# State products of both heads in one 128-column product, behind the half's masked-score products

## The chip, the cores and the metric

The kernel runs on one core of one Trainium2 chip. The metric is the device time in microseconds of one execution. A core has TensorE (in the profile PE, its weight loads PEld), VectorE (DVE), ScalarE (ACT), GpSimd (POOL) and the DMA queues, of which SyncE (SP) issues most here. Each engine works through its own instructions in the order written; semaphores tie the engines together.

## The reference

Decay attention in blocks, then a mixer. The shapes are 4 batches, 8 heads, 768 positions and 64 dimensions per head; the mixer has 256 token features and 1536 channel features.

```python
for b in range(nb):                      # blocks of 64 positions
    intra = einsum('bhic,bhjc->bhij', qb, kb) * Dmask      # masked scores
    intra = einsum('bhij,bhjd->bhid', intra, vb)
    inter = einsum('bhid,bhde->bhie', qb * lam_pow, kv_state)
    out[:, :, sl] = intra + inter
    kv_state = lam_block * kv_state + einsum('bhsd,bhse->bhde', kb * rev_pow, vb)
...
u = x + (relu(x.T @ w_tok1) @ w_tok2).T
return u + relu(u @ w_ch1) @ w_ch2
```

## The kernel before

The attention works on 16 **pairs**: one batch and two neighbouring heads (h = 0, 1), whose 64 dimensions fill 128 partitions. Positions are cut into 6 chunks of 128. The six chunks are two **halves** of three, g = 0 and 1.

For pair i, `scores` makes the 128x128 scores of every chunk and VectorE multiplies them by the decay mask (tile `a`, L299). `state` makes the products of decayed k with v (`kv`, L257), VectorE scans them over the chunks (`sv`, L265), and GpSimd places them in `st` (program name `stb`, L278): for every chunk 128x128, head 0's state in rows and columns 0 to 63, head 1's in 64 to 127, zeros elsewhere. GpSimd also scales q (`qs`, L244). `outputs(i, g)` then adds up in one PSUM bank `xT`, which has 3x128 columns, head h in partitions 64h to 64h+63: for every chunk and head the masked-score product (L314: v as weights, 64 columns, `a` streamed) and, but for chunk 0, the state product (L324: the head's 64 columns of `st` as weights, all 128 rows, `qs` streamed). ScalarE copies the bank to `uT` (L331). There is one `xT` bank, so the other half's first product waits for that copy.

The order is the one in which the code is written, for all engines. A pass of the loop over i issues: scores of pair i+1, `outputs(i, 0)`, the `kv` products of pair i+1, `outputs(i, 1)`, then transposes of k and q of pair i+2 (L208, L228; from pair 5 and 8 on VectorE and DMAs do these: L218, L221), then from pass 4 on pieces of the token mixer (`token_hidden` L449, `token_out` L469), with the transposes of the finished half (`turn_back`, L346) between them. In pass 15 there is no `kv`; a `token_hidden` stands between the two halves. Loads of later pairs and of the mixer's weights go through SP. The channel mixer (L640, L661) follows from about 179 us to the end.

Of the kernel before, what the change touches and what calls it, by code (L numbers as in the profile page):

```python
# [21 lines left out]
def kernel(  # L22
# [23 lines left out]
    nc = tc.nc  # L46
    B, H, S, D = q.shape
# [3 lines left out]
    P = 128  # L51
# [27 lines left out]
    def bank(tag, nm, n):  # L79
        return ps.tile([P, n], F32, tag=tag, bufs={"sc": 4, "xT": 1, "sh": 3}[tag], name=nm)  # L80
# [99 lines left out]
    for i in range(2):  # L180
        st = ap.tile([P, NC - 1, 2, D], F32, name=f"stb{i}")
# [7 lines left out]
    while n < P:  # L189
        nc.vector.tensor_mul(  # L190
            out=lamp[:, :, n : 2 * n], in0=lamp[:, :, 0:n], in1=lamp[:, :, n - 1 : n].broadcast_to([P, NP, n])
        )
        n *= 2
    for p in range(NP):
        nc.gpsimd.tensor_copy(
            out=keep[:, p, :, 1:], in_=lamp[:, p, P - 1 : P, None].broadcast_to([P, D, NC - 2])
# [3 lines left out]
    kTs, qTs, qss, kds, weights_of = {}, {}, {}, {}, {}  # L200
# [105 lines left out]
    def outputs(i, g):  # L306
        b, p = pairs[i]
        st = stb[i % 2]
        xT = bank("xT", f"xT{i}{g}", 3 * P)
        for cg in range(3):  # L310
            c = 3 * g + cg
            cs = slice(cg * P, (cg + 1) * P)
            for h in range(2):
                nc.tensor.matmul(  # L314
                    out=xT[h * D : (h + 1) * D, cs],
                    lhsT=vns[i][:, h, c, :],
                    rhs=weights_of[i, g, h][:, cg, :],
                    start=(cg == 0),
                    stop=False,
                )  # L320
            if c == 0:
                continue
            for h in range(2):
                nc.tensor.matmul(  # L324
                    out=xT[h * D : (h + 1) * D, cs],
                    lhsT=st[:, c - 1, h, :],
                    rhs=qss[i][:, c - 1, :],
                    start=False,
                    stop=(cg == 2),
                )  # L330
        nc.scalar.copy(out=uT[b][:, p, 3 * g * P : (3 * g + 3) * P], in_=xT)  # L331

    x_of = {}
# [221 lines left out]
    for i in range(-2, NI):  # L555
# [3 lines left out]
        if i >= 0:  # L559
            outputs(i, 0)  # L560
# [4 lines left out]
        if i >= 0:  # L565
            outputs(i, 1)
# [201 lines left out]
```

## Time and profile before

| | us |
|---|---|
| three runs | 600.35, 600.77, 603.7 |
| their median | 600.77 |
| the profiled execution | 602.27 |
| its span, first to last instruction | 600.5 |
| VectorE, ScalarE, GpSimd busy in the span | 349.3, 155.4, 139.0 |

In the profile a group of instructions is named by its line, engine and operation, then out<-in with the program's names, the part of the TensorE array that it uses (128\*64 is all 128 rows and 64 columns), the shape and the count. An fp32 matmul is recorded as two instructions (two passes), so that the 160 state products are x320. "Mean ns of one" is from start to modelled end; matmuls overlap, so their rate is read from starts.

### The profile page before, as it was taken

To read this page: it belongs to the slowest core of one execution; us is meant where nothing else is said; L and a number is where in the kernel's file an instruction comes from. 1 tells how busy PE (TensorE), PEld (TensorE's weight loads), DVE (VectorE), ACT (ScalarE), POOL (GpSimd) and SP (SyncE) were. 2 spreads that over 40 slices of the span, in tenths; PEclk is the share of its full clock that TensorE was granted. 3 is DMA by queue.
4 is the path that set the end of the run, shared out by engine and by line. 5 is a ranking of instruction groups with operands and counts; after the bars stand their busy time and mean duration, and the time that the engine had idled before them with its cause. 6 is when DMAs were issued, how large, how long until landed. Compare 5 with 4: busy or idle time off the path is not lost.

```text
span 600.5 us, 10671 instructions
## 1 busy us (share of the span) xinstructions
PE 581.5 (97%) x4378; PEld 566.3 (94%) x4378; DVE 349.3 (58%) x663; ACT 155.4 (26%) x322; POOL 139.0 (23%) x131
## 2 busy tenths in 40 slices
PE   5979899999999999999999999999999999999997
PEld 5868799889999999999999999999999999999996
DVE  4588777886733667446534664446534664356654
ACT  3454423444223243212201221012211221011011
POOL 5646533364215358201100010001100010000000
PEclk9989899999999999999999999999999999999999
DMA  9999899999100112011200111011200200016667
GB/s 186 240 229 172 140 175 164 191 175 161 37 11 27 37 36 70 1 33 38 71 1 0 61 47 35 1 36 41 66 1 0 71 1 1 0 21 90 89 90 134
DMA packets 169648, 44.73 MB, mean 74 GB/s; under 512 B 162816, under 2 KB 163968, under 8 KB 169600
## 3 DMA queue, kind: packets, MB, share of 16 engines
q1 hardware_dynamic: 165456, 42.88, 37.6%
q10 hardware_dynamic: 4144, 1.18, 0.9%
q8 instruction: 34, 0.56, 0.4%
q14 instruction: 14, 0.11, 0.1%
HBM read 37.75 MB, written 6.29 MB: 73 GB/s over the span
## 4 chain that ended last, share of the span: by engine, by line
PE 87%; DVE 6%; DMA 4%; ACT 2%; issue 1%; SPq 0%; ACTq 0%; DVEq 0%
PE ph L640 34%; PE po L661 33%; PE ph L449 6%; PE pu L469 4%; PE xT L314 3%; PE sc L290 3%; PE xT L324 2%; DMA kn<-in_k_dram 2%; DMA uT<-in_moe_w_tok_dram 2%; PE xp L346 1%; DVE xlo L355 1%; PE kv L257 1%; DVE uT L383 1%; DVE a L299 1%; DVE uT L389 1%
## 5 line engine op out<-in xcount | busy, mean ns | idle before, releaser
L645 DVE SCALAR_TENSOR_TENSOR hl<-ph,hh 128x384 fp32r<-128x384 f32 x96 | 53.5, 558 | 164.9 <-ACT hh L644 164.9
L661 PE MATMUL po<-hh,c2h 128*128 128x384 f32 x384 | 129.4, 337 | 0.0
L640 PE MATMUL ph<-uh,c1h 128*128 128x384 f32 x384 | 129.2, 337 | 0.0
L640 PE MATMUL ph<-ul,c1h 128*128 128x384 f32 x384 | 129.2, 336 | 0.0
L640 PE MATMUL ph<-uh,c1l 128*128 128x384 f32 x384 | 129.1, 336 | 0.0
L661 PE MATMUL po<-hh,c2l 128*128 128x384 f32 x384 | 128.8, 335 | 0.0
L661 PE MATMUL po<-hl,c2h 128*128 128x384 f32 x384 | 128.6, 335 | 0.0
L644 ACT ACTIVATE hh<-ph 128x384 fp32r<-128x384 f32 x96 | 47.3, 492 | 299.5 <-PE ph L640 297.8
L666 DVE TENSOR_TENSOR uT<-po,uT 128x384 f32<-128x384 f32 x192 | 104.7, 552 | 23.5 <-PE po L661 23.4
L661 PEld LDWEIGHTS po<-hh,c2l 128*128 128x128 f32 x384 | 72.1, 188 | 0.0
L640 PEld LDWEIGHTS ph<-ul,c1h 128*128 128x128 f32 x384 | 72.1, 188 | 0.0
L661 PEld LDWEIGHTS po<-hl,c2h 128*128 128x128 f32 x384 | 72.1, 188 | 0.0
L640 PEld LDWEIGHTS ph<-uh,c1h 128*128 128x128 f32 x384 | 72.1, 188 | 0.0
L661 PEld LDWEIGHTS po<-hh,c2h 128*128 128x128 f32 x384 | 72.0, 188 | 0.0
L640 PEld LDWEIGHTS ph<-uh,c1l 128*128 128x128 f32 x384 | 72.0, 188 | 0.0
L375 POOL TENSOR_TENSOR c1l<-wa,c1h 128x512 fp32r<-128x512 f32 x10 | 12.9, 1292 | 179.9 <-ACT c1h L374 179.9
L534 POOL TENSOR_TENSOR ul<-uT,uh 128x384 fp32r<-128x384 f32 x32 | 36.0, 1157 | 37.4 <-ACT uh L533 37.4
L314 PE MATMUL xT<-a,vn 128*64 128x128 f32 x384 | 37.1, 285 | 4.3 <-ACT uT L331 4.3
L278 POOL COPY stb<-sv 64x320 f32<-64x320 f32 x32 | 26.7, 834 | 43.6 <-DVE sv L265 42.7
L299 DVE TENSOR_TENSOR a<-sc,mask 128x384 f32<-128x384 f32 x64 | 31.2, 549 | 5.8 <-PE sc L290 5.7
L324 PE MATMUL xT<-qs,stb 128*64 128x128 f32 x320 | 32.0, 278 | 0.0
L314 PEld LDWEIGHTS xT<-a,vn 128*64 128x64 f32 x384 | 22.8, 139 | 8.3 <-ACT uT L331 4.7
(80 smaller groups left out, 756.9 us busy)
## 6 DMA issues: line engine op xcount, KB each, us to landing
raw<-in_moe_w_ch_dram SPq DMA_DIRECT2D x20, 512.0 KB, 3.6
vn<-in_v_dram SPq DMA_DIRECT2D x16, 384.0 KB, 5.4
kn<-in_k_dram SPq DMA_DIRECT2D x30, 192.0 KB, 5.3
out_dram<-y SPq DMA_DIRECT2D x108, 48.0 KB, 1.9
qn<-in_q_dram SPq DMA_DIRECT2D x44, 96.0 KB, 4.1
uT<-in_moe_w_tok_dram SPq DMA_DIRECT2D x2, 1536.0 KB, 8.5
kr<-in_k_dram SPq DMA_DIRECT2D x32, 96.0 KB, 4.1
uT<-in_moe_w_ch_dram SPq DMA_DIRECT2D x4, 512.0 KB, 5.3
```

The costliest lines, as they stand in the source:

```text
L278: nc.gpsimd.tensor_copy(out=st[r, :, h, :], in_=sv[r].rearrange("p (e c) -> p c e", c=NC - 1))
L299: nc.vector.tensor_mul(out=a, in0=sc[h].rearrange("p (c i) -> p c i", i=P), in1=mask[:, 2 * p + h, None, :].broadcast_to([P, 3, P]),)
L314: nc.tensor.matmul(out=xT[h * D : (h + 1) * D, cs], lhsT=vns[i][:, h, c, :], rhs=weights_of[i, g, h][:, cg, :], start=(cg == 0), stop=False,)
L324: nc.tensor.matmul(out=xT[h * D : (h + 1) * D, cs], lhsT=st[:, c - 1, h, :], rhs=qss[i][:, c - 1, :], start=False, stop=(cg == 2),)
L449: nc.tensor.matmul(out=ph, lhsT=w[:, c, fs], rhs=x[:, c], start=(i == 0), stop=(i == 3 * NC - 1))
L469: nc.tensor.matmul(out=pu, lhsT=h[:, kk, cs], rhs=w[:, kk, ss], start=(i == 0), stop=(i == 3 * NK - 1))
L534: nc.gpsimd.tensor_sub(out=ul[:, t], in0=ub[:, t], in1=uh[:, t].bitcast(F32))
L640: nc.tensor.matmul(out=ph, lhsT=w[:, ct, js], rhs=x[:, ct], start=(i == 0), stop=(i == 11))
L644: nc.scalar.activation(hh, ph, AF.Relu)
L645: nc.vector.scalar_tensor_tensor(out=hl, in0=ph, scalar=0.0, in1=hh.bitcast(F32), op0=ALU.max, op1=ALU.subtract)
L661: nc.tensor.matmul(out=po, lhsT=w[:, jj, cs], rhs=h, start=(i == 0), stop=(i == 3 * JG - 1))
L666: nc.vector.tensor_add(out=ub, in0=po, in1=ub)
```

## The change

In a half, the state products no longer stand between the chunks' masked-score products, one for each head. A loop of its own behind the three chunks makes them with one product per chunk for both heads: all 128 columns of `st` are the weights, and the result goes to all 128 partitions of `xT`. What is computed is the same, since the parts of `st` off the two blocks are zeros.

```diff
-            if c == 0:
-                continue
-            for h in range(2):
-                nc.tensor.matmul(
-                    out=xT[h * D : (h + 1) * D, cs],
-                    lhsT=st[:, c - 1, h, :],
-                    rhs=qss[i][:, c - 1, :],
-                    start=False,
-                    stop=(cg == 2),
-                )
+        for c in range(max(3 * g, 1), 3 * g + 3):
+            cs = slice((c - 3 * g) * P, (c - 3 * g + 1) * P)
+            nc.tensor.matmul(
+                out=xT[:, cs],
+                lhsT=st[:, c - 1].rearrange("p h d -> p (h d)"),
+                rhs=qss[i][:, c - 1, :],
+                start=False,
+                stop=(c == 3 * g + 2),
+            )
         nc.scalar.copy(out=uT[b][:, p, 3 * g * P : (3 * g + 3) * P], in_=xT)
```

The state product is L324 before and L323 in the changed kernel, whose lines behind it are one lower (L449 becomes L448). Only TensorE's order changes; the other engines and queues have the same instructions in the same order.

TensorE in pair 8, the end of half 0 and the step to half 1. `xT80` and `xT81` are the banks of the two halves, `a800` and `a801` the masked scores of the two heads; before:

```order
L314 MATMUL xT80_1383<-a801_1210,vn8_1036 64x128
L314 MATMUL xT80_1383<-a800_1208,vn8_1036 64x128
L314 MATMUL xT80_1383<-a801_1210,vn8_1036 64x128
L324 MATMUL xT80_1383<-qs8_1224,stb0_111 64x128 x2
L314 MATMUL xT80_1383<-a800_1208,vn8_1036 64x128
L314 MATMUL xT80_1383<-a801_1210,vn8_1036 64x128
L324 MATMUL xT80_1383<-qs8_1224,stb0_111 64x128 x2
L257 MATMUL kv9_1395<-vn9_1184,kd9_1290 64x64 x10
L314 MATMUL xT81_1408<-a810_1220,vn8_1036 64x128
```

and the same place in the changed kernel:

```order
L314 MATMUL xT80_1343<-a800_1173,vn8_1006 64x128
L314 MATMUL xT80_1343<-a801_1175,vn8_1006 64x128
L314 MATMUL xT80_1343<-a800_1173,vn8_1006 64x128
L314 MATMUL xT80_1343<-a801_1175,vn8_1006 64x128
L323 MATMUL xT80_1343<-qs8_1189,stb0_111 128x128 x2
L257 MATMUL kv9_1353<-vn9_1149,kd9_1250 64x64 x10
L314 MATMUL xT81_1366<-a810_1185,vn8_1006 64x128
```

Two products of 128 columns stand directly ahead of `kv` in the place of four of 64 columns; before them all products of the half have 64 columns, and `kv` behind them has 64 again.

TensorE in pair 8, the end of half 1 and the token mixer's first products behind it (`ph101`); before:

```order
L314 MATMUL xT81_1408<-a810_1220,vn8_1036 64x128
L314 MATMUL xT81_1408<-a811_1222,vn8_1036 64x128
L324 MATMUL xT81_1408<-qs8_1224,stb0_111 64x128 x2
L449 MATMUL ph101_1430<-xhi10_853,w1h_129 128x256
L449 MATMUL ph101_1430<-xhi10_853,w1l_130 128x256
```

and changed:

```order
L314 MATMUL xT81_1366<-a810_1185,vn8_1006 64x128
L314 MATMUL xT81_1366<-a811_1187,vn8_1006 64x128
L323 MATMUL xT81_1366<-qs8_1189,stb0_111 128x128 x3
L448 MATMUL ph101_1385<-xhi10_828,w1h_129 128x256
L448 MATMUL ph101_1385<-xhi10_828,w1l_130 128x256
```

The step from 64-column to 128-column products stood ahead of the mixer's products; it now stands three state products earlier.

## The prediction

> **What bounds the kernel now.** First the page: busy shares, then the chain that ended last.
>
> ```profile
> PE 581.5 (97%) x4378; PEld 566.3 (94%) x4378; DVE 349.3 (58%) x663; ACT 155.4 (26%) x322; POOL 139.0 (23%) x131
> PE 87%; DVE 6%; DMA 4%; ACT 2%; issue 1%; SPq 0%; ACTq 0%; DVEq 0%
> ```
>
> TensorE is 87% of the chain, so a change of its work counts, unless TensorE then waits less. The state products all lie before 179 us. The view by stretches shows how tight TensorE is there (columns: length, busy us and instructions by engine, granted clock, DMA).
>
> ```profile
> 20.60:54.00 33.40, 28.46 (x408) 24.84 (x408) 26.09 (x47) 16.79 (x38) 19.29 (x17) 0.95 1.02 228
> 76.00:182.00 106.00, 104.94 (x1224) 97.03 (x1221) 74.49 (x136) 37.13 (x81) 38.17 (x36) 1.00 0.81 131
> ```
>
> From 76 us on TensorE is busy 104.94 of 106 us: pairs 6 to 15 are bound by it. In 20.6 to 54 us it is free for some 5 us: pairs 1 to 4 run under another bound.
>
> Next the timeline of TensorE over pair 8 (start, length, line, part of the array, count).
>
> ```profile
> 98.83 0.66 PE L314 MATMUL xT<-a,vn 128*64 128x128 f32 x8
> 99.31 0.39 PE L324 MATMUL xT<-qs,stb 128*64 128x128 f32 x4
> 99.53 0.39 PE L314 MATMUL xT<-a,vn 128*64 128x128 f32 x4
> 99.75 0.39 PE L324 MATMUL xT<-qs,stb 128*64 128x128 f32 x4
> 99.97 0.75 PE L257 MATMUL kv<-vn,kd 128*64 128x64 f32 x20
> 100.72 0.44 PE L314 MATMUL xT<-a,vn 128*64 128x128 f32 x4
> ...
> 101.86 0.39 PE L324 MATMUL xT<-qs,stb 128*64 128x128 f32 x4
> 102.18 0.39 PE L449 MATMUL ph<-xhi,w1h 128*128 128x256 f32 x1
> 102.40 0.28 PE L449 MATMUL ph<-xhi,w1l 128*128 128x256 f32 x1
> 102.52 0.28 PE L449 MATMUL ph<-xlo,w1h 128*128 128x256 f32 x1
> ```
>
> Groups of four (two heads, two passes) start 0.22 us apart. The same timeline, cut to a narrow window, shows two of them, and the costliest groups have the length of one (count, busy us, mean ns):
>
> ```profile
> 99.42 0.28 PE L324 MATMUL xT<-qs,stb 128*64 128x128 f32 x2
> ...
> L324 PE MATMUL xT<-qs,stb 128*64 128x128 f32 x320 | 32.0, 278 | 0.0
> L257 PE MATMUL kv<-vn,kd 128*64 128x64 f32 x320 | 12.6, 223 | 1.1 <-ACT kd L237 0.6 <-POOL kd L239 0.5
> ```
>
> Two instructions together take 0.28 us, and one alone 278 ns, so **both heads' passes start together**, each on its half of the columns. A chunk's state product costs two passes of 0.11 us, not four.
>
> **What the change does to the passes.** The 128-column product has two passes as well, and each streams the same 128 columns of `qs`. The trace has no fp32 product of this form. Bounds: the weights of 128 columns and 128 streamed columns of the scores, twelve steps of two heads in 1.54 us, 0.13 each with the start-up in them and 0.12 with the 0.2 for it taken off (the entry price worked out below); on the other side half of 0.11, if four passes' work really went away. I take 0.11 per pass, the pace of L314 and L324, since the streamed side is the same and the scores' weights, as wide, hold their pace near it.
>
> ```profile
> 97.36 1.54 PE sc L290 x24
> ```
>
> **Gain in the passes: 0.** 160 instructions go, but their time lay beside the other head's.
>
> **What it adds: changes of the array's form.** The last L324 pass starts at 101.97 (0.11 after 101.86), the first L449 at 102.18: 0.21 where a pass takes 0.11. The second L449 follows after 0.22, where 0.12 is its pace (102.40 to 102.52): its weights are not loaded ahead. So entering the 128-column form costs 0.10 + 0.10 = 0.20 us. The Trainium skill, "TensorEngine Tiling (Array Packing)", Key Properties, says that a change of mode, as against a change of tile, drains the engine; the 0.21 here agrees, and it speaks against this change; it names no price. With transposes behind, entry is cheaper:
>
> ```profile
> 45.74 0.39 PE L324 MATMUL xT<-qs,stb 128*64 128x128 f32 x4
> 46.06 0.44 PE L208 MATMUL kt<-ident,kn 128*128 128x128 f32 x2
> ```
>
> 45.85 to 46.06 is again 0.21, but the second follows after 0.44 - 0.28 = 0.16, against 0.11 in steady state: 0.10 + 0.05, about 0.16 with rounding. For L323, a full product like L449 and not a transpose, I take 0.20; 0.16 is the lower end, and would take 0.4 off the sum below.
>
> Leaving the 128-column form is seen at pair 15:
>
> ```profile
> 172.91 0.28 PE L449 MATMUL ph<-xlo,w1h 128*128 128x256 f32 x1
> 173.12 0.66 PE L314 MATMUL xT<-a,vn 128*64 128x128 f32 x8
> ```
>
> 0.21 instead of 0.12, and eight instructions in 0.66 where four steps would give 3 x 0.11 + 0.28 = 0.61: 0.09 + 0.05 = 0.14 us.
>
> **Half 0, pairs 0 to 14**: one entry (0.20) before the state products and one exit (0.14) into `kv`, both new. The exit has cover. `kv`'s last pass starts at 100.50 (99.97 + 0.75, less 0.22 for the last one), and its steps are 0.06, so half 1 could start at 100.56; it starts at 100.72, behind ScalarE's copy of the one `xT` bank:
>
> ```profile
> 100.19 0.48 ACT L331 COPY uT<-xT 128x384 f32<-128x384 f32 x1 [2.41 <-PE xT L324]
> ```
>
> The copy ends at 100.67. It hangs on the last state product, not on `kv`, so 0.14 of exit goes into 0.16 of wait. Without that cover it would cost its 0.14. The scan behind `kv` comes 0.34 later, with the next pair's half 0 to use it several us on.
>
> **Half 1**: the entry that stood ahead of the next work moves three products up. Before L208 or L346 (pairs 0 to 5, 11, 12, 15) 0.20 replaces 0.16: +0.04. Before L449 or L469 (6 to 10, 13, 14) +0. **Pair 15**: no `kv`; in half 0 the entry moves only, 0. In half 1 the copy is awaited by a transpose, and the copy comes the whole 0.20 later:
>
> ```profile
> 178.81 0.31 PEld L346 LDWEIGHTS xp<-ident,uT 128*128 128x128 f32 x3 [0.34 <-ACT uT L331]
> ```
>
> **What waits swallow.** From the chain in order of time, the timeline of TensorE, and that of its weight loads:
>
> ```profile
> 20.59 9.87 DMA uT<-in_moe_w_tok_dram
> 35.08 0.69 PE L314 MATMUL xT<-a,vn 128*64 128x128 f32 x4 [2.22 <-ACT uT L331]
> 44.60 0.44 PE L314 MATMUL xT<-a,vn 128*64 128x128 f32 x4 [0.88 <-ACT uT L331]
> 52.48 0.44 PE L314 MATMUL xT<-a,vn 128*64 128x128 f32 x4 [1.23 <-ACT uT L331]
> 63.14 0.74 PE L257 MATMUL kv<-vn,kd 128*64 128x64 f32 x17 [0.48 <-POOL kd L239]
> 68.25 0.55 PE L346 MATMUL xp<-ident,uT 128*128 128x128 f32 x3 [2.20 <-DVE sv L265]
> 86.41 3.70 DMA qn<-in_q_dram
> 94.94 0.19 PEld L449 LDWEIGHTS ph<-xhi,w1h 128*128 128x128 f32 x1 [0.40 <-DVE uT L474]
> 117.29 6.57 DMA kn<-in_k_dram
> 129.49 0.31 PEld L346 LDWEIGHTS xp<-ident,uT 128*128 128x128 f32 x3 [0.56 <-issue]
> ```
>
> Pair 1 and half 0 of pair 2 lie beside the load of 20.59 and the conversion behind it, which end in the wait of 2.22; half 0 of pair 3 in 0.88; its half 1 and half 0 of pair 4 in 1.23; pair 5 in 0.48 and 2.20. Pairs 7 (about 88 us) and 10 (about 122) lie beside the loads of 86.41 and 117.29, with TensorE waiting 0.40 and 0.56 at their ends. Pair 0 stands before the load of 20.59 on the chain, and 6, 8, 9, 11 to 14 on TensorE's own stretch of it.
>
> **Sum.** Eight pairs at 0.20 = 1.6; five half 1s before transposes on the chain (0, 2, 4, 11, 12) at 0.04 = 0.2; pair 15 0.2: **+2.0 us**. On the profiled execution 602.27 + 2.0 = 604.3; it is 1.5 over the median of 600.77, so on the median **602.8**. Its own uncertainty: in two stretches the clock was granted at half,
>
> ```profile
> 34.66:38.07 3.41, 2.99 (x25) 2.66 (x26) 3.38 (x6) 0.48 (x2) 3.34 (x3) 0.50 0.93 182
> 68.80:72.20 3.40, 3.40 (x18) 3.40 (x18) 1.16 (x3) 1.51 (x3) 3.26 (x4) 0.50 1.19 150
> ```
>
> in the second with TensorE fully busy: 18 instructions in 3.40 us, at 0.12 each 2.2. One such stretch more or less is some 1.3 us, with the pass price of 0.12 for 0.11 (about 0.6 over the paying pairs) 1.5: 601.3 to 604.3.
>
> **Rivals.** *Fewer instructions are worth their time*: a pass costs an issue price, so a chunk falls from 0.22 to 0.11. Eight full pairs then give 8 x (0.55 - 0.20) = 2.8, the half 1s of 2 and 4 2 x 0.29, pair 15 0.35: -3.6 after the small terms, 597.2. The Trainium skill's same page, Instruction Overhead, has some 60 cycles for each matmul on TRN2, which points this way. Against: the two heads in 0.28 us, above. 6%.
>
> *Everything follows TensorE* (the slower side): the waits above are released by work that TensorE fed a few us before, so they move along instead of swallowing, and `kv`, late by 0.34, becomes what half 1 waits for. It decides where an exit costs over 0.16 or the delay between two waits exceeds the second (0.40 is the smallest). Then all 15 pairs pay 0.34, nine half 1s 0.04, pair 15 0.2: +5.6, 606.4. For it: 0.14 is close to 0.16. Against: the two loads and conversions of 2 to 10 us have their own length. 16%.
>
> *No weights ahead*: a full fp32 pass can't have the next weights loaded beside it, 0.22 instead of 0.11 for each pass after the first; about eight per pair and eight pairs +7, with half 1 of 2, 4 and 15 +8.4, so 611. Against: the scores at 0.12 with weights as wide. 4%.
>
> *No drain*: widening from 64 to 128 columns with the same rows costs nothing: 600.8. Against: 102.18. 4%.
>
> **Chances.** The forecast has 70%. A measurement tells 0.5% from no change, that is 3.0 us: 597.8 and 603.8. Of the forecast's range a sixth, 0.12, lies over 603.8. Slower: 0.12 + 0.16 + 0.04 = 0.32; same: 0.58 + 0.04 = 0.62; faster 0.06. The range reaches over the second rival and stops short of the first and third: 600.6 to 606.4.
>
> **What would show it.** L323 x160, starts 0.11 apart, 0.21 after the last L314 and 0.21 again to its second pass; `kv` 0.21 after the last L323; half 1's first L314 still 0.05 behind the copy's end; no change after 180 us. Wrong if L323 runs at 0.06 or 0.22 a pass, if half 1 starts behind `kv` alone, or if the waits at 35, 52, 68, 95 and 129 us keep their lengths while their ends move later.

## The result, and the profile after

| | us |
|---|---|
| changed kernel, 7 runs | 602.77 to 606.82, median 604.48 |
| kernel before, the 7 runs beside it | 599.93 to 603.7, median 600.77 |
| ratio | 1.0071, 95% interval 1.0046 to 1.0096 |
| the same comparison again (7 runs; 18 of before) | 1.0054, 1.0035 to 1.0073 |

The change makes the kernel slower by 4.3 us (2.8 to 5.8), or 3.2 (2.1 to 4.4) in the second comparison, each ratio taken on 600.77. The direction was forecast and the size was too small: +2.0. The median lies 0.7 us over 603.8, where the prediction had set the bound between no change (chance 0.62) and slower (0.32).

The profiled execution of the changed kernel took 604.34 us, its span is 602.6. The page's busy line and the chain:

```profile
PE 584.3 (97%) x4218; PEld 566.1 (94%) x4218; DVE 349.4 (58%) x663; ACT 154.7 (26%) x322; POOL 138.9 (23%) x131
PE 87%; DVE 5%; DMA 4%; ACT 1%; SPq 1%; POOL 0%; issue 0%; POOLq 0%
```

160 instructions are gone and TensorE is busy 2.8 us longer. The timeline of TensorE over pair 8, to be laid beside the one of before:

```profile
98.37 0.88 PE L314 MATMUL xT<-a,vn 128*64 128x128 f32 x12
99.18 0.71 PE L323 MATMUL xT<-qs,stb 128*128 128x128 f32 x4
99.82 0.80 PE L257 MATMUL kv<-vn,kd 128*64 128x64 f32 x20
100.46 0.88 PE L314 MATMUL xT<-a,vn 128*64 128x128 f32 x12
101.27 0.94 PE L323 MATMUL xT<-qs,stb 128*128 128x128 f32 x6
101.96 0.36 PE L448 MATMUL ph<-xhi,w1h 128*128 128x256 f32 x1
102.16 0.28 PE L448 MATMUL ph<-xhi,w1l 128*128 128x256 f32 x1
```

Half 0 takes 100.46 - 98.37 = 2.09 us, before 100.72 - 98.83 = 1.89: +0.20, as predicted. Half 1 to the mixer's second product takes 102.16 - 100.46 = 1.70, before 102.40 - 100.72 = 1.68. ScalarE's copy between the halves:

```profile
99.93 0.48 ACT L330 COPY uT<-xT 128x384 f32<-128x384 f32 x1 [2.60 <-PE xT L323]
```

It ends at 100.41 and half 1 starts at 100.46, 0.05 behind it as before. But `kv`'s last pass now starts at 100.40 (99.82 + 0.80 - 0.22), and with its step of 0.06 half 1 could start at 100.46 behind `kv` alone, too: both are ready together, the exit has filled the wait.

The clock differs between the two profiles, and any comparison of spans has to know it (stretches, columns as before):

```profile
34.30:37.70 3.40, 2.65 (x27) 2.31 (x27) 3.40 (x6) 1.57 (x5) 3.00 (x3) 1.00 1.29 220
68.41:71.82 3.41, 3.41 (x19) 3.41 (x18) 1.21 (x4) 1.47 (x4) 2.88 (x3) 0.50 1.32 163
```

The stretch at 34.66 that had half the clock before has all of it here. So the spans differ by 2.1 us only, while the timed runs differ by 3 to 4.

To see where TensorE loses time, take the start of each pair's first masked-score product (the first L314 behind its scores), in a kernel less in the kernel before, and from that the step from one pair to the next. This is what each pair costs (us):

```
pair                 6    7    8    9   10   11   12   13  14+15   sum
predicted          .20    0  .20  .20    0  .24  .24  .20    .40   1.68
changed            .25  .37  .21  .21  .38  .28  .26  .22    .43   2.61
changed, again     .25  .36  .21  .20  .35  .28  .26  .22    .43   2.56
half 1 alone       .01  .00  .01  .01  .02  .07  .08  .03    .21    .44
half 0 alone       .19  .36  .19  .19  .38  .20  .19  .21    .21   2.12
order alone        .03 -.01 -.01 -.01  .00  .00  .00  .03    .01    .04
```

The column 14+15 is the step from pair 14 to the channel mixer's first L661. Pairs 7 and 10 stand out. Pairs 0 and 1, which the table leaves out, cost 0.31 us each in both profiles of the changed kernel, where the prediction had 0.24 and 0.

The prediction also named waits (at 35, 52, 68, 95 and 129 us) that would show it wrong if they kept their lengths. These are they, with two more of its list, at the times of before and in us; those at 95 and 129 are waits of TensorE's weight loads:

```
wait at             35    44    52    63    68    95   129
before            2.22   .88  1.23   .48  2.20   .40   .56
changed           2.14   .64   .97  none  2.14   .49   .59
changed, again    2.22   .53   .96  none  2.14   .49   .58
```

Those at 44, 52 and 63 us gave up 0.24 to 0.48 us. Those at 35 and 68 kept their lengths to 0.08 us, and those at 95 and 129, the ends of pairs 7 and 10, got no shorter at all.

### The profile page after: what moved, and what is told of

It is laid out like the page before. It is cut to its first block, busy times and chain, and to the rows that moved or that the text cites. A ratio compares the mean times of both kernels' runs of the same rounds, so it can differ in the third digit from the quotient of the medians.

```text
span 602.6 us, 10351 instructions
## 1 busy us (share of the span) xinstructions
PE 584.3 (97%) x4218; PEld 566.1 (94%) x4218; DVE 349.4 (58%) x663; ACT 154.7 (26%) x322; POOL 138.9 (23%) x131
## 4 chain that ended last, share of the span: by engine, by line
PE 87%; DVE 5%; DMA 4%; ACT 1%; SPq 1%; POOL 0%; issue 0%; POOLq 0%
PE ph L639 33%; PE po L660 33%; PE ph L448 6%; PE pu L468 4%; PE xT L314 3%; PE xT L323 3%; PE sc L290 2%; DMA uT<-in_moe_w_tok_dram 2%; DMA qn<-in_q_dram 1%; PE kv L257 1%; PE xp L345 1%; DMA kn<-in_k_dram 1%; DVE a L299 1%; DVE xlo L354 1%; DVE uT L391 1%; DMA kr<-in_k_dram 1%
## 5 line engine op out<-in xcount | busy, mean ns | idle before, releaser
L314 PE MATMUL xT<-a,vn 128*64 128x128 f32 x384 | 28.1, 281 | 3.8 <-ACT uT L330 3.8
L330 ACT COPY uT<-xT 128x384 f32<-128x384 f32 x32 | 15.3, 479 | 60.4 <-PE xT L323 60.4
L448 PE MATMUL ph<-xhi,w1h 128*128 128x256 f32 x96 | 28.8, 300 | 0.5 <-DVE hl L453 0.3
```

The costliest lines, as they stand in the source:

```text
L314: nc.tensor.matmul(out=xT[h * D : (h + 1) * D, cs], lhsT=vns[i][:, h, c, :], rhs=weights_of[i, g, h][:, cg, :], start=(cg == 0), stop=False,)
L448: nc.tensor.matmul(out=ph, lhsT=w[:, c, fs], rhs=x[:, c], start=(i == 0), stop=(i == 3 * NC - 1))
```

## The experiments

All experiments but the repetition put the state products of one chunk into a function `states(cg)` and choose with two flags: `wide` takes one 128-column product in the place of two of 64 columns, `behind` calls it behind the half's masked-score products and not behind each chunk's. The kernel before is `False, False`, the change `True, True`. The cuts below are of this code (`...` marks what is left out).

**Order alone.** The state products behind the masked-score products, but still one per head:

```diff
+        wide, behind = False, True
...
+            if not behind:
+                states(cg)
+        if behind:
+            for cg in range(3):
+                states(cg)
```

> State products moved behind the half's masked-score products, but still two of 64 columns per chunk. Theory A (the price is changing the array's form, 128*64 to 128*128 and back): no form is changed more often than before, so +0 us, within 1 us of the kernel before; in the trace the half is 0.22 us per chunk and product as before. Rival B (the new order itself costs, since the bank's last products now hang on the states): +2 to +4 us, like the whole change.

602.51 us against 601.78, ratio 1.0011 (0.9989 to 1.0033). In the trace no late pair moves by over 0.04 us (last row of the table of pairs). A holds: the new order is free, so the cost is in the widening.

**Wide, in place.** One 128-column product behind each chunk's masked-score products:

```diff
+        wide, behind = True, False
```

> One 128-column state product per chunk, left in its old place behind that chunk's masked-score products, so that the form changes at every chunk. Theory A, with 0.20 us to enter and 0.14 us to leave: half 0 pays 0.34 + 0.20 (its last exit lies in the wait for the copy), half 1 0.34 + 0.34 + 0.04, some 1.24 us per pair; the ten to eleven pairs on TensorE's path give +13 to +14 us, all sixteen +19.5. Theory C (the 128-column pass itself is dearer, by 0.01 to 0.02 us, and the form is free): as the whole change, +2 to +4 us.

615.46 against 601.78, ratio 1.024 (1.0211 to 1.0269): +14.4 us, where A gave 13 to 14 and C 2 to 4. As many 128-column passes as in the change cost over three times as much, so the price is on the change of form. TensorE in half 0 of pair 8 and the step to half 1 (in the experiments' kernels the masked-score products are L339, the 128-column state products L318, the 64-column ones L327):

```profile
100.98 0.66 PE L339 MATMUL xT<-a,vn 128*64 128x128 f32 x8
101.57 0.49 PE L318 MATMUL xT<-qs,stb 128*128 128x128 f32 x2
101.99 0.44 PE L339 MATMUL xT<-a,vn 128*64 128x128 f32 x4
102.36 0.49 PE L318 MATMUL xT<-qs,stb 128*128 128x128 f32 x2
102.78 0.80 PE L257 MATMUL kv<-vn,kd 128*64 128x64 f32 x20
103.42 0.44 PE L339 MATMUL xT<-a,vn 128*64 128x128 f32 x4
```

103.42 - 100.98 = 2.44, 0.55 over the 1.89 of before; worked out had been 0.34 + 0.20.

**Half 1 alone, half 0 alone.** The change in one half, the old code in the other (one line for each kernel):

```diff
+        wide, behind = g == 1, g == 1
...
+        wide, behind = g == 0, g == 0
```

> Half 1 as in the change, half 0 as before. Half 1 ends in 128-column work anyway, so the form changes as often as before. Theory A: +0.04 us before transposes, 0 before the token mixer, 0.2 in pair 15: +0.4 us in all. Theory C (each 128-column pass dearer): three fifths of the change's cost, +1.2 to +2.6 us.

> Half 0 as in the change, half 1 as before. Theory A: 0.20 us in each pair that TensorE bounds and nothing for the exit, which lies in the wait for the copy: +1.6 us if waits swallow what the prediction says, +3 us if all 15 pairs pay; nearly the whole cost of the change either way. Theory C: two fifths of the change's cost, +0.8 to +1.7 us.

Half 1: 603.08 against 601.78, 1.0019 (0.9995 to 1.0042). Half 0: 605.86, 1.0069 (1.0048 to 1.0089), all of the change's cost, +4.1 us (2.9 to 5.3). In the table the two rows add up to the changed kernel's sum: 0.44 + 2.12 = 2.56. Theory C, with three and two fifths, falls by half 0, whose interval begins over C's 1.7; half 1's, -0.3 to 2.5, would allow it. A's +3 for half 0, "if all 15 pairs pay", lies in the interval, but the pairs do not pay alike: pairs 7 and 10 cost 0.36 and 0.38, from half 0.

**Why pairs 7 and 10.** VectorE around pair 10, and the wait of TensorE at the pair's end, before and in the changed kernel:

```profile
123.12 0.82 DVE L265 TENSOR_TENSOR_SCAN sv<-keep,kv 128x320 f32<-128x320 f32 x1 [0.63 <-PE kv L257]
123.86 0.95 DVE L218 STREAM_TRANSPOSE qT<-qn 128x768 f32<-128x768 f32 x1
...
129.52 0.52 PE L346 MATMUL xp<-ident,uT 128*128 128x128 f32 x3 [0.26 <-DVE uT L474]
```

```profile
123.44 0.82 DVE L265 TENSOR_TENSOR_SCAN sv<-keep,kv 128x320 f32<-128x320 f32 x1 [0.98 <-PE kv L257]
124.18 0.95 DVE L218 STREAM_TRANSPOSE qT<-qn 128x768 f32<-128x768 f32 x1
...
129.84 0.52 PE L345 MATMUL xp<-ident,uT 128*128 128x128 f32 x3 [0.30 <-DVE uT L473]
```

VectorE waits for `kv`, scans, and only then transposes q and k of pair 12 and does the conversions and the additions (L474) that TensorE waits for at 129.52. The transpose starts right behind the scan in both. `kv` ends later by the whole 0.34, entry and exit, and here no copy covers the exit. From the pair's start (121.11 and 121.08) the scan comes 0.35 later and so does the end of TensorE's wait, 8.76 us behind the start and not 8.41. So the wait at the end of the pair does not swallow; it moves.

The chain of waits had named a load (117.29, 6.57 us) whose landing fell at the start of the transpose. That load fills `kn`, and the transposes of VectorE read `qn` (L218) and `kr` (L221), so they had no need of it. The loads of q for pair 12 (the eighth group of four, since pair 5 is the first) were issued long before, and a load of this kind takes 4.1 us to land in the median. In pair 7 it is the same: the load of q that the chain names (86.41) belongs to the sixth group, that of pair 10, while VectorE transposes pair 9 there. The loads of pair 12:

```profile
108.98 3.26 SPq L104 DMA_DIRECT2D qn<-in_q_dram  x4
```

The test moves VectorE's transposes ahead of the scan in the changed kernel:

```diff
+        if i + 2 < NI:
+            turn_q(i + 2)
         place = state(i + 1) if 0 <= i + 1 < NI else None
...
             outputs(i, 1)
-        if i + 2 < NI:
-            turn_q(i + 2)
```

> The changed kernel with VectorE's transposes of q and k of pair i+2 ahead of the scan behind kv, not behind it. If the waits of pairs 7 and 10 hang on kv through the scan (A2), TensorE no longer waits 0.4 to 0.6 us at their ends: 0.7 to 1.3 us less than the changed kernel, and the transposes start up to 1 us earlier. If they hang on the loads of q and k, as the prediction read the chain, the transposes start as late as now and nothing is gained.

```profile
122.43 1.95 DVE L299 TENSOR_TENSOR a<-sc,mask 128x384 f32<-128x384 f32 x4 [0.28 <-PE sc L290]
124.30 0.97 DVE L218 STREAM_TRANSPOSE qT<-qn 128x768 f32<-128x768 f32 x1
125.19 0.94 DVE L221 STREAM_TRANSPOSE kT<-kr 128x768 f32<-128x768 f32 x1
126.05 0.78 DVE L265 TENSOR_TENSOR_SCAN sv<-keep,kv 128x320 f32<-128x320 f32 x1
...
127.94 0.56 DVE L494 TENSOR_TENSOR uT<-pu,uT 128x384 f32<-128x384 f32 x1 [0.79 <-PE pu L489]
```

The pair starts at 123.00 here. The transpose starts 1.30 us behind that; in the changed kernel 124.18 - 121.08 = 3.10. So the loads do not hold the transposes back, and the prediction's reading of the chain was wrong. Pair 10 costs 0.27 instead of 0.38, pair 7 0.30 instead of 0.37. They do not come free, since VectorE now waits 0.79 us for the token mixer's product `pu` (last line), whose first matmul TensorE starts 0.23 later in the pair than before (126.58 - 123.00 = 3.58, before 124.46 - 121.11 = 3.35). TensorE's wait at the pair's end stays and ends 8.68 us behind the pair's start (131.68): as far as this trace shows, it is fed by TensorE's own work either way. The expected gain in time did not come: 606.77 against 602.18, 1.0077 (1.0047 to 1.0108). In pair 4 the transposes do wait for a load, and the scan and all behind it with them:

```profile
53.16 0.98 DVE L218 STREAM_TRANSPOSE qT<-qn 128x768 f32<-128x768 f32 x1 [1.88 <-DMA qn<-in_q_dram]
```

That pair loses 2.44 us. So A2's mechanism is shown, that `kv` reaches TensorE through the scan and VectorE's order; its gain of 0.7 to 1.3 us was not had, of which pairs 7 and 10 gave back 0.18.

**The changed kernel again.**

> The changed kernel once more, beside the next three. Theory A2 (two changes of form per pair, 0.20 to enter and 0.14 to leave; the exit is hidden from half 1 by the copy, but not from VectorE, whose scan waits for kv): +3 to +4 us, pairs 7 and 10 at +0.37 each and the other late pairs at +0.21 to +0.28. The sum as predicted (pairs 7 and 10 free): +2.0. Also looked at: the time from the last product to the end, 5.1 us from the last channel product in the profile of before and 5.7 in that of the changed kernel. If that is a draw of the execution it is near 5.1 here as often as not; if the change makes it, it is 5.6 or more.

605.72 against 602.18, +3.2 us (2.1 to 4.4), with the steps of the table, pairs 7 and 10 at 0.36 and 0.35. It fits A2, and the predicted +2.0 lies just under the interval. The end of the span, 5.5 us from the last channel product, lies between the two cases and decides nothing by itself.

**In place, early or late pairs alone.** The costly form in five pairs each (one line for each kernel):

```diff
+        wide, behind = 1 <= i <= 5, False
...
+        wide, behind = 11 <= i <= 15, False
```

> In pairs 1 to 5 alone, a 128-column product at every chunk's old place, some 1.24 us more TensorE time in each, 6.2 in all; the other pairs as before. If the waits of these pairs (2.2, 0.9, 1.2, 0.5 and 2.2 us before) swallow it: 0 to +2 us. If everything there follows TensorE: +6 us.

> The same in pairs 11 to 15 alone, where TensorE waits for nothing: 4 x 1.24 + 1.2 = +6.2 us by either theory, if 0.20 and 0.14 are the prices.

Early: 602.19 against 602.18, 1.0012 (0.9995 to 1.0028). Late: 608.77, 1.0112 (1.0091 to 1.0133), +6.7 us; in the trace pairs 11 to 15 cost 1.32 + 1.29 + 1.24 + 2.49 = 6.3. The same added work costs 6.7 us at the end and 0.7 at the beginning (-0.3 to 1.7).

But the waits swallow only a part of it; the rest is hidden by the clock. Ten of the twelve runs with the early pairs had a mean granted clock of 0.998 or more and took 601.0 to 602.5 us. None of the 18 runs of before beside them was above 0.997: three at 0.997 took 600.6 us in the mean, seven at 0.994 took 602.4. That is some 0.6 us for each 0.001 of clock, so that before would take some 599.6 us at the mean clock of these ten, which took 601.9. By this estimate 2.3 of the 6.2 us were paid, and the waits swallowed some 4. (In the second comparison the changed kernel and before had the same mean clock, 0.994, so there the clock hides nothing.)

**Two banks.** The copy's wait, and with it the cover of the exit, goes when `xT` has two PSUM banks; first the kernel before, then the changed one:

```diff
-        return ps.tile([P, n], F32, tag=tag, bufs={"sc": 4, "xT": 1, "sh": 3}[tag], name=nm)
+        return ps.tile([P, n], F32, tag=tag, bufs={"sc": 4, "xT": 2, "sh": 2}[tag], name=nm)
```

> The kernel before with two PSUM banks for xT (and two in the place of three for the group that kv, the transposes and the token products use). Half 1 no longer waits for half 0's copy: the 0.16 us of wait per pair goes, -1.6 us over the ten pairs that show it, if two banks are enough for the rest. If they are not, TensorE waits there, more than it gains.

> The changed kernel with the same two banks. Without the wait for the copy the exit from the 128-column form (0.14) is no longer covered: from half 0 to half 1 the changed order costs 0.34 per pair against the two-bank kernel before, where it costs 0.20 with one bank. Against that kernel, the sum over the late pairs is 1 to 1.5 us more than the changed kernel's over the kernel before, +4.5 to +5 us. If the exit costs nothing anywhere, the two differences are equal.

The first is 613.2 against 601.15, 1.0208 (1.0182 to 1.0234): two banks for the rest are not enough. The weight loads' waits show it, the first line in the kernel before, the others with two banks:

```profile
PEld pu L469 <- DVE uT L474: 0.5, 1, 0.5
...
PEld kt L208 <- DVE sv L265: 7.9, 5, 2.7
PEld pu L489 <- DVE uT L494: 6.1, 10, 0.8
```

The second is 618.34, 1.0281 (1.0255 to 1.0307), 5.1 us more by the medians. TensorE in pair 8 of the first and of the second, from half 0 to half 1:

```profile
102.58 0.66 PE L339 MATMUL xT<-a,vn 128*64 128x128 f32 x8
...
103.72 0.75 PE L257 MATMUL kv<-vn,kd 128*64 128x64 f32 x20
104.31 0.39 PE L339 MATMUL xT<-a,vn 128*64 128x128 f32 x4
```

```profile
101.93 0.88 PE L339 MATMUL xT<-a,vn 128*64 128x128 f32 x12
102.74 0.71 PE L318 MATMUL xT<-qs,stb 128*128 128x128 f32 x4
103.38 0.80 PE L257 MATMUL kv<-vn,kd 128*64 128x64 f32 x20
104.01 0.83 PE L339 MATMUL xT<-a,vn 128*64 128x128 f32 x12
```

1.73 us and 2.08: +0.35, entry and exit; with one bank it was +0.20. The 1.73 is also 0.16 less than the 1.89 of one bank, the wait for the copy. Every pair from 6 to 13 now costs 0.34 to 0.43 against the two-bank kernel before and pairs 7 and 10 (0.36 and 0.34) are like the rest. The late pairs sum to 3.56, 0.95 over the 2.61 of one bank, where 1 to 1.5 had been expected. The cover was real: without the copy's wait the 0.14 of the exit is paid.

## Why the prediction was right or wrong

- **No gain in the passes: right.** L323 starts 0.11 us apart (its group of six is 0.94 long: 0.21 to the second, 4 x 0.11, and 0.28). Two heads' passes had run together before.
- **Price of the form, 0.20 to enter and 0.14 to leave: right.** 99.82 less the last L323 start (99.18 + 0.21 + 2 x 0.11 = 99.61) is 0.21 again, and wide-in-place, with five products per pair, cost 1.19 to 1.32 in pairs 6 to 13, where 1.24 had been worked out from the two prices.
- **The exit lies in the wait for the copy: right for half 1, wrong for VectorE.** The prediction said that "the scan behind `kv` comes 0.34 later, with the next pair's half 0 to use it several us on". It named the scan's consumer and not what is queued behind the scan on VectorE: the transposes, conversions and additions that TensorE waits for in pairs 7 and 10.
- **Waits swallow pairs 1 to 5: right in part.** The waits at 44, 52 and 63 us shrank, those at 35 and 68 hardly. With 6.2 us added to these pairs the time rose by 0.7, but some 1.6 us of what is missing (2.3 - 0.7) are the clock's, which the prediction did not see.
- **Pairs 7 and 10 free: wrong**, 0.37 and 0.38 instead of 0: 0.75 of the 0.93 us by which the late pairs' sum was too small (2.61 against 1.68). This is the step that failed. The prediction took the loads that the chain named for what bounds these pairs; VectorE waited for `kv` there, and the waits at 95 and 129 us moved instead of shrinking, which the prediction itself had named as a sign of being wrong.
- **Half 1 before transposes, +0.04: too small**: 0.07 and 0.08 in pairs 11 and 12, 0.12 and 0.11 in pairs 0 and 1 (half 1 alone). What makes the difference between these pairs was not tried. **Pair 15**, 0.20: right, 0.21.
- **The rivals.** "Everything follows TensorE" (606.4) was half right: it holds in pairs 7 and 10, and the timed result lies between it and the forecast; but in pairs 3 to 5 waits did swallow, and the exit into half 1 stays covered. The forecast's own terms gave 601.3 to 604.3; the 604.48 lies inside the stated 600.6 to 606.4 only since that range was drawn over this rival. No gain from fewer instructions, no missing weight prefetch (0.11 a pass), and the drain is there (the 0.21).
- **What stays open.** The late pairs give 2.6 us, the runs 3.2 to 4.3; the interval of the second comparison holds 2.6, that of the first just misses it. Two parts of the execution can hold the rest. One is the early pairs: in the second profile of the changed kernel, whose two stretches of half clock lie about where they lie before (35.7 and 69.8 us), pairs 0 to 5 lose 0.79, of which pairs 0 and 1 0.31 each. The other is the end: from the start of the last channel product (L661) to the end of the span it takes 5.1 us in the four profiles without wide products in half 0, 5.7 and 5.5 in the two of the changed kernel, 5.6 to 6.8 in five others with wide products there. In that second profile the two together account for the span: 2.56 + 0.79 + 0.37 at the end, less 0.28 ahead of pair 0, is 3.44 of 3.45 us. But neither is shown to come from the change. With the order alone, where nothing is added, pair 2 moved by 0.96 in its profile; and the end takes no more than 5.2 in the changed kernel with two banks. One or two profiles per kernel do not tell whether the change shifts the odds.

## What to carry to other kernels

Before joining two half-width products into one, look whether they start together in the trace: then the join saves nothing, and every step between column widths has a price (here 0.20 us into 128 columns and 0.14 back). Put such steps where a step stands anyway (half 1 here), not into the middle of a run of narrow products. For each delayed instruction, list what is queued behind its consumer on that engine, too: a load that the chain names as the release may only have landed at the same moment. Look whether the waiting instruction reads what that load fills, and when its own loads were issued.

## What the runs showed of the hardware that was not expected

Added TensorE work in the early pairs raised the granted clock. With five wide products in each of pairs 1 to 5, ten of twelve runs had a mean clock of 0.998 or more, and with them in all pairs all six had 0.997 to 0.999; with them in pairs 11 to 15 alone the five runs had 0.992 to 0.997, like the kernel before beside them. In the profiles the kernel before has two stretches of 3.4 us at half clock, the one with wide products in all pairs none before the end. That shorter waits of TensorE are the reason is likely and was not tried. So times of two kernels whose mean clocks differ hold two effects: here 0.7 us in the medians was some 2.3 at equal clock.
